# Left tiles of a top-1 expert layer: expert weights split once into 16-bit parts in memory, and left rows grouped by expert over pairs of batches

## The chip, the cores and the metric

The kernel runs on one core of one Trainium2 chip. The metric is the device time of one execution in microseconds (us). The core's engines are called PE (TensorE, matmuls and the weight loads in front of them), ACT (ScalarE), DVE (VectorE), POOL (GpSimd) and SP (which only issues DMAs here). Each engine works through its own instructions in order and waits on semaphores for the others.

## The reference

Agent attention with 49 agents over four batches of 11456 tokens with 128 channels gives one vector per token. A gate picks one of eight experts for each token, and the expert (128 to 1024 to 128, with a relu between) is applied and scaled.

```python
a2k = sm(agents, k)              # softmax of scale * agents @ k^T
agent_v = a2k @ v                # 49 x 128 per batch
q2a = sm(q, agents)
x = (q2a @ agent_v)              # one row of 128 per token, 45824 rows

logits = x @ w_gate
e_idx = np.argmax(logits, axis=1)
gate_w = softmax(logits)[row, e_idx]
eom = 1 / (1 + np.exp(-(x @ w_output_gate)))
for e in range(8):
    mask = e_idx == e
    h = np.maximum(x[mask] @ w1[e], 0)
    out[mask] = gate_w[mask, None] * eom[mask, e, None] * (h @ w2[e])
```

With the reference's inputs nearly all tokens of a batch go to one expert, the batch's dominant one. The others, the left rows, are few: 705 in batch 0 (677 for expert 3, 27 for expert 4, 1 for expert 1), 432 in batch 1 (431 for expert 4, 1 for expert 7), none in batch 2 and 37 in batch 3 (expert 4).

## The kernel before

The **main stream** computes every token with its batch's dominant expert. A batch is 12 units of eight tiles of 128 tokens, the last one short; a unit is two groups of 512 tokens. Per group, `mm1` makes the hidden values in two halves of four PSUM banks (`h`, 512 wide, f16), `relu` writes a 16-bit high part with ACT (`hh`) and a low part with DVE (`hl`), and `mm2` multiplies both with the split second weights (`vv`): a 256-wide product for `hh` and a 128-wide one for `hl` into `y`. `finish` adds the parts with ACT (`ys`) and DVE (`os`), and POOL scales the rows by `smt` ahead of the store. The scores of k and q (`ks`, `qs`), the averages (`av`) and the gate logits (`lg`) are small products that are slipped in between. For q, `q_rest` makes the exponentials `ef`, of which a copy goes to memory (`efd`) together with the token's gate factor in column 49.

The **left rows** are worked out afterwards. `left_table` counts the left rows per group and makes a table of tiles of up to 128 rows of one group; `left_index` finds the tokens of some tiles, and POOL gathers their `ef` rows. `left_load` has SP read the tile's averages (`lav`) and its expert's weights (`lw_ld`, f32, 512 KB each) from memory. `left_front` turns the `ef` rows (`let`, copied by ACT to `let_sb`) and multiplies them with the averages (`lx`, copied to `lxs`). `left_back` makes eight f32 products of 128 columns for the hidden layer (`lh`), relu on ACT, and eight f32 products for the output (`ly`); ACT scales the result, and POOL scatters its rows into `out`. A group is an expert in one batch. `PHASES` fixes the tiles that are laid out in the program: 13 for batches 0 to 2 and one for batch 3; more than these would be worked in a loop at the end.

Nothing of the order is left to the hardware: the builder keeps a clock of its own with a cost for each instruction, and every piece of work is a generator in `streams` with a priority. `tick`, `block` and `idle` let those go on whose operands are ready by that clock, between the instructions of `main_stream`. A changed cost, priority or condition moves instructions on all engines. `left_static` runs two ways of left tiles, `left_scatter` writes their rows, `choose` loads a batch's dominant expert, `kept` writes a batch's averages to memory, and `q_tail` counts.

## Time and profile before

| what | value |
|---|---|
| median of three runs | 976.56 us (976.25 to 977.01) |
| the profiled execution's own time | 976.57 us |
| its span in the trace | 974.8 us |
| mean granted clock of PE | 0.997 |
| first main hidden product (`h`) | 57.3 us |
| first and last left product (`lh`, `ly`) | 779.4 and 965.2 us |
| bytes moved by DMA | 148.63 MB |
| loads of left weights (`lw_ld`) | 28 of 512 KB |

A row of the profile names an engine, an operation, the tiles it writes and reads (out<-in) and its shape as partitions x elements. Since a helper records every operation, all have line 219, and rows are told apart by their tiles. In a row of time the first number is the start in us from the start of the span, the second the time from the first to the last of the xN instructions that it merges, and a bracket names the idle time ahead and what ended it. An f32 product counts as two records. "median" columns of a tile's rows are min/median/max in ns; rows with a bar give busy us in total and mean ns of one, then the idle time before it.

### The profile page before, as it was taken

What the parts mean: (1) busy time and instruction counts of PE and PEld (TensorE: products, weight loads), DVE (VectorE), ACT (ScalarE), POOL (GpSimd) and SP (SyncE); (2) the same over time, 40 slices, a digit from 0 to 9 for tenths busy, and PEclk for the clock granted to TensorE, in tenths of its full rate; (3) what the DMA queues carried; (4) which work ended last, traced back from release to release, by engine and by line L of the source; (5) the groups of instructions that cost most, each with busy time, mean ns of one, the idle gap of its engine ahead of it and who ended that gap; (6) DMA issues with size and microseconds to landing.
All of it is one profiled execution on the core that took longest, in us unless ns stands there. A gap on an engine that the chain in (4) does not pass through costs nothing. (4 is left out here: it accounts for less than half of the span.)

```text
span 974.8 us, 37665 instructions
## 1 busy us (share of the span) xinstructions
PE 953.0 (98%) x15819; PEld 730.4 (75%) x15819; DVE 788.0 (81%) x2119; ACT 590.5 (61%) x1401; POOL 352.5 (36%) x629
## 2 busy tenths in 40 slices
PE   9999999999999999999999999999999999999996
PEld 7867777777777777776777777777777677888885
DVE  2878888989888887889878889889999878678652
ACT  2366666665766666667666666667566566555552
POOL 1013255552232364431323554521234354442221
PEclk9999999999999999999999999999999999999998
DMA  9986655646465655444566545444333453825420
GB/s 332 297 295 162 162 148 156 154 140 172 150 185 155 176 159 137 148 133 146 143 182 172 155 133 161 148 133 135 103 82 83 119 144 96 195 77 163 165 73 29
DMA packets 108899, 148.63 MB, mean 152 GB/s; under 512 B 62595, under 2 KB 71223, under 8 KB 108725
## 3 DMA queue, kind: packets, MB, share of 16 engines
q1 hardware_dynamic: 107380, 144.70, 51.5%
q8 instruction: 125, 2.05, 0.9%
q0 software_dynamic: 1344, 1.49, 0.8%
q14 instruction: 50, 0.40, 0.1%
HBM read 90.88 MB, written 35.17 MB: 129 GB/s over the span
## 5 line engine op out<-in xcount | busy, mean ns | idle before, releaser
L219 PE MATMUL y<-vv,hh 128*128 128x256 f16 (+1 forms) x2880 | 526.6, 273 | 5.2 <-DVE lL L219 2.3
L219 DVE SCALAR_TENSOR_TENSOR hl<-h,hh 128x512 f16<-128x512 f32 (+1 forms) x736 | 448.1, 667 | 93.1 <-ACT hh L219 90.7
L219 PE MATMUL y<-vv,hl 128*128 128x128 f16 (+1 forms) x2880 | 500.0, 219 | 1.5 <-DVE hl L219 0.9
L219 ACT ACTIVATE hh<-h 128x512 f16<-128x512 f32 (+1 forms) x736 | 372.1, 590 | 185.1 <-PE h L219 184.8
L219 PEld LDWEIGHTS <-hh 128*128 128x128 f16 (+1 forms) x2880 | 282.7, 98 | 56.9 <-issue 16.0
L219 PEld LDWEIGHTS <-hl 128*128 128x128 f16 (+1 forms) x2880 | 283.8, 99 | 9.5 <-issue 4.4
L219 PE MATMUL h<-x_ld,w 128*128 128x512 f16 (+1 forms) x1472 | 256.2, 376 | 0.7 <-DVE hl L219 0.4
L219 PEld LDWEIGHTS <-w 128*128 128x128 f16 x1472 | 83.5, 95 | 109.4 <-issue 72.9
L219 POOL TENSOR_TENSOR os<-os,smt 128x512 f32<-128x512 f32 (+1 forms) x91 | 94.9, 1042 | 114.1 <-DVE os L219 65.2
L219 ACT COPY ys<-y 128x256 f32<-128x256 f32 x179 | 67.6, 378 | 103.4 <-PE y L219 101.7
L219 DVE TENSOR_TENSOR os<-y,ys 128x256 f32<-128x256 f32 x179 | 74.2, 414 | 29.2 <-ACT ys L219 25.3
L219 POOL TENSOR_TENSOR e<-ef,e 128x392 f16<-128x392 f32 (+1 forms) x48 | 43.2, 899 | 67.8 <-ACT e L219 67.7
L219 POOL TENSOR_TENSOR ev<-S,km_o 128x400 f32<-128x400 f32 (+1 forms) x36 | 32.8, 914 | 58.2 <-PE av L219 53.9
L219 PEld LDWEIGHTS ks<-at,k_ld 128*32 128x32 f32 (+1 forms) x2316 | 39.9, 116 | 10.3 <-issue 7.8
L219 PE MATMUL ks<-at,k_ld 128*32 128x50 f32 (+1 forms) x2316 | 46.6, 213 | 0.7 <-DMA k_ld<-kT 0.6
L219 PE MATMUL qs<-at,q_ld 128*32 128x50 f32 (+1 forms) x2736 | 43.3, 210 | 0.0
L219 PEld LDWEIGHTS qs<-at,q_ld 128*32 128x32 f32 (+1 forms) x2736 | 36.5, 111 | 9.0 <-issue 8.0
L219 PE MATMUL lh<-lxs,lw_ld 128*128 128x128 f32 x224 | 42.5, 276 | 0.7 <-ACT lh L219 0.6
L219 PE MATMUL ly<-lw_ld,lh 128*128 128x128 f32 x224 | 42.3, 276 | 0.0
L219 POOL TENSOR_SCALAR smt<-lT,i 128x8 f32<-128x8 f32 (+1 forms) x48 | 15.5, 323 | 70.5 <-DVE lT L219 41.6
L219 POOL TENSOR_TENSOR og<-oh,ll 128x64 f32<-128x64 f32 (+1 forms) x48 | 16.3, 340 | 66.7 <-DVE oh L219 47.0
L219 ACT COPY S<-ks 128x400 f32<-128x400 f32 (+1 forms) x48 | 23.5, 490 | 23.2 <-PE ks L219 23.2
(252 smaller groups left out, 1012.8 us busy)
## 6 DMA issues: line engine op xcount, KB each, us to landing
v_ld<-v SPq DMA_DIRECT2D x44, 512.0 KB
q_ld<-qT SPq DMA_DIRECT2D x44, 512.0 KB
out<-os SPq DMA_DIRECT2D x88, 256.0 KB
k_ld<-kT SPq DMA_DIRECT2D x43, 512.0 KB
lw_ld<-w SPq DMA_DIRECT2D x28, 512.0 KB
efd<-ef SPq DMA_DIRECT2D x44, 200.0 KB
x_ld<-x_ld SPq DMA_DIRECT2D x132, 64.0 KB
w1t<-w SPq DMA_DIRECT2D x4, 512.0 KB
```

The lines of the kernel that those rows point to most:

```text
L219: return getattr(self.eng, op)(*a, **k)
```

## The change

1. `PHASES` pairs the batches: phase 0 is batches 0 and 1 with 12 tiles, phase 1 batches 2 and 3 with one. A group is now an expert over both batches of a pair, with the count of the first batch (`cnt0`) kept in the table, so that a row's batch follows from its place (`two`, a 0/1 column per batch). The averages of both batches are one tile of 98 rows, loaded once per phase, and the `ef` row stands in the half of its batch (`xt`, DVE).
2. `halves` reads each expert's two weight matrices once, scales them by a power of two from the sum of squares, splits them into 16-bit high and low parts, and writes them to memory (`w1p`, `w2p`). Three experts are split in each of the batches 0 and 1 and two in batch 2, at priority 3.
3. The left tiles load these parts (the bytes are the same) and use three f16 products instead of one f32 product for the hidden layer, and a 256-wide and a 128-wide one for the output. The values between are split too (`lxs`, `lh`: high part on ACT, low part on DVE), the result is put together by ACT and DVE, and the powers of two are undone in the row factor (`lg`, and `sxi` in `ef`).
4. Priorities: the last q units of batch 3 and the preparing of phase 1 go to 0.

```diff
-PHASES = [(0, 3, 13, 384), (3, 1, 1, 128)]
+PHASES = [(0, 2, 12, 256), (2, 2, 1, 256)]
...
-        yield from ACT.q.copy(avn[0:A], t[0:A, 0:P])
+        sx, state[b]["sxi"] = yield from scale(state[b]["an"], f"sx{b}", 4)
+        yield from ACT.q.activation(avn[0:A], t[0:A, 0:P], AF.Copy, scale=sx[0:A])
...
+    def halves():
+        for e in range(E):
+            while not (clk.started and len(state) > e // 3 and "i12" in state[len(state) - 1]
+                       and (len(state) < B and K.get(len(state), {"v": 0})["v"] < 8) and not urgent[0]):
+                yield None
+            halving[0] = True
+            src, dst = [], []
+            for x in (w1, w2):
+                s = wk.tile([P, F], F32, name=f"hw{len(src)}_{e}", tag="w1t", bufs=2)
+                yield from SY.q.dma_start(s, x[e])
+                src.append(s)
...
+                yield from ACT.q.activation(d[:, 0:F], src[k], AF.Square, accum_out=sq[:, k:k + 1])
...
+            yield from PE.q.matmul(r[:, 0:2], ones, sq, start=True, stop=True)
...
+                yield from ACT.q.activation(full, full, AF.Copy, scale=s[:, k:k + 1])
+                yield from ACT.q.copy(hi, full)
+                yield from POOL.q.tensor_tensor(lo, full, hi, op=ALU.subtract)
+                yield from SY.q.dma_start(x[e], dst[k])
+            halved[0] = e + 1
+            halving[0] = False
...
-        spawn(q_rest(b, u, s, mark))
+        spawn(q_rest(b, u, s, mark), LASTQ if b == B - 1 and u >= 10 else 2)
...
-        yield from POOL.q.tensor_copy(ef[0:pp, 0:nt, A], T)
+        yield from POOL.q.tensor_scalar(ef[0:pp, 0:nt, A], T, state[b]["sxi"][0:pp], None, op0=ALU.mult)
...
-            yield from PE.q.matmul(t[:, 0:n * P], ones[0:ng, :], c[0:ng].rearrange("p n k -> p (n k)"), start=True,
-                                   stop=True)
+            for k in range(n):
+                yield from PE.q.matmul(t[:, k * P:(k + 1) * P], c[0:ng, k, :], ppt[0:ng], start=True, stop=True)
...
-        yield from SY.q.dma_start(w1t, w1[bass.ds(er, 1)].rearrange("a p f -> p (a f)"))
+        yield from SY.q.dma_start(w1t, w1p[bass.ds(er, 1)].rearrange("a p f -> p (a f)"))
...
+        yield from DVE.q.tensor_tensor(xt, ef[:, 0:A].unsqueeze(1).broadcast_to([P, 2, A]),
+                                       two.unsqueeze(2).broadcast_to([P, 2, A]), op=ALU.mult)
...
-        yield from PE.q.transpose(t[0:A, 0:P], ef[:, 0:A], idf)
+        yield from PE.q.transpose(t[0:2 * A, 0:P], xt.rearrange("p b k -> p (b k)"), idf)
...
-        yield from ACT.q.copy(xs, x[:, 0:P])
+        yield from ACT.q.copy(xs[:, 0, :], x[:, 0:P])
+        yield from DVE.q.scalar_tensor_tensor(xs[:, 1, :], x[:, 0:P], 1.0, xs[:, 0, :], op0=ALU.mult, op1=ALU.subtract)
...
-                yield from PE.q.matmul(h[:, j * P:(j + 1) * P], w1t[:, fs], xs, start=True, stop=True)
+                yield from PE.q.matmul(d, w1t[:, f0:f0 + P], xs[:, 0, :], start=True, stop=False)
+                yield from PE.q.matmul(d, w1t[:, f0:f0 + P], xs[:, 1, :], start=False, stop=False)
+                yield from PE.q.matmul(d, w1t[:, F + f0:F + f0 + P], xs[:, 0, :], start=False, stop=True)
...
-            yield from ACT.q.activation(hs, h, AF.Relu)
+            yield from ACT.q.activation(hs[:, 0, :], h, AF.Relu)
+            yield from DVE.q.scalar_tensor_tensor(hs[:, 1, :], h, 0.0, hs[:, 0, :], op0=ALU.max, op1=ALU.subtract)
...
+            yield from PE.q.matmul(y[:, 0:2 * C], hs[:, 0, fs], w2v[:, f, :], start=(f == 0), stop=False)
+            yield from PE.q.matmul(y[:, 0:C], hs[:, 1, fs], w2v[:, f, 0:C], start=False, stop=(f == NB - 1))
-        yield from ACT.q.activation(o, y[:, 0:C], AF.Copy, scale=ef[:, A:A + 1])
+        yield from ACT.q.activation(o, y[:, C:2 * C], AF.Copy, scale=g)
+        yield from DVE.q.scalar_tensor_tensor(o, y[:, 0:C], g, o, op0=ALU.mult, op1=ALU.add)
...
-        while counted[0] < b0 + nb:
+        while counted[0] < (3 if ph == 0 else B) or ph and not prepared[0]:
...
-        for j, n in enumerate((3, 4, 4, 2) if nst > 2 else (nst,)):
+        for j, n in enumerate((4, 4, 4) if nst > 2 else (nst,)):
...
-                while (ph, k) not in ready or i > finished[0]:
+                while (ph, k) not in ready or i > finished[0] or halved[0] < E:
...
-        spawn(left_prepare(ph), 1)
+        spawn(left_prepare(ph), 1 - ph)
...
+    spawn(halves(), 3)
```

Where the instructions stand now. First ACT in batch 1, at the second half of a main group: `hh` are the relus of the main stream, `S` and `ys` copies of scores and outputs, `e` the 16-bit exponentials. Before:

```order
L219 ACTIVATE hh_0_6423<-h_0_0_6400 128x512
L219 ACTIVATE hh_1_6426<-h_0_1_6410 128x512
L219 ACTIVATE hh_2_6429<-h_0_2_6412 128x512
L219 ACTIVATE hh_3_6431<-h_0_3_6417 128x512
L219 CAST e_3_90<-ef_3_6394 128x8x49
L219 COPY S_3_6477<-ks_3_6337 128x400
L219 ACTIVATE hh_4_6538<-h_1_0_6521 128x512
```

And in the changed program, where `hw` is an expert's matrix and `hd` its parts:

```order
L219 ACTIVATE hh_0_6516<-h_0_0_6494 128x512
L219 ACTIVATE hh_1_6519<-h_0_1_6500 128x512
L219 ACTIVATE hh_2_6522<-h_0_2_6502 128x512
L219 ACTIVATE hh_3_6524<-h_0_3_6510 128x512
L219 COPY S_3_6568<-ks_3_6409 128x400
L219 ACTIVATE hw_3_6121<-hw_3_6121,hs_6414 128x1024
L219 CAST hd_3_6126<-hw_3_6121 128x1024
L219 ACTIVATE hh_4_6624<-h_1_0_6608 128x512
```

Two instructions of 1024 columns stand between the two groups of four relus, and the cast of `e` has moved away.

Next PE at the end of the program, from the last products of the main stream on. Before, the second half of one left tile follows (tile 0 of the last phase, whose `let` and `lx` stand earlier), and then the branches of the loop at the end:

```order
L219 MATMUL y_0_21469<-vv_1_15806,hh_7_21427 96x256
L219 LDWEIGHTS hl_7_21428
L219 MATMUL y_0_21469<-vv_1_15806,hl_7_21428 96x128
L219 MATMUL lh_0_0_21508<-lxs_0_21396,lw_00_0_ld 128x128 x4
L219 MATMUL lh_0_1_21519<-lxs_0_21396,lw_00_0_ld 128x128 x4
L219 MATMUL ly_0_21528<-lw_00_0_ld,lh_0_0_21516 128x128 x4
L219 MATMUL ly_0_21528<-lw_00_0_ld,lh_0_1_21525 128x128 x4
```

In the changed program tile 10 of the first phase only starts there with its `lx`:

```order
L219 MATMUL y_0_21790<-vv_1_15990,hh_7_21702 96x256
L219 LDWEIGHTS hl_7_21703
L219 MATMUL y_0_21790<-vv_1_15990,hl_7_21703 96x128
L219 MATMUL lx_10_21818<-let_sb_10_21814,lav_16750 128x128
L219 LDWEIGHTS lw_100_0_ld
L219 MATMUL lh_10_0_21843<-lxs_10_21834,lw_100_0_ld 128x128
```

Behind it come the rest of tile 10, all of tile 11 and all of the last phase's tile; ten left tiles stand ahead of the last main product, where it was 13 before.

Last DVE at the same place in the changed program (there were no left rows on DVE behind the main stream before): the low parts of `lh`, the `xt` products (in `big`, 98 columns) and the outputs (in `big`, from `ly`):

```order
L219 SCALAR_TENSOR_TENSOR lh_10_0_21860<-lh_10_0_21843,lh_10_0_21860 128x512
L219 TENSOR_TENSOR big_8_19745<-big_8_19745,ltwo_8s_8_19908 128x98
L219 SCALAR_TENSOR_TENSOR lh_10_1_21876<-lh_10_1_21863,lh_10_1_21876 128x512
L219 SCALAR_TENSOR_TENSOR lxs_11_21895<-lx_11_21883,lxs_11_21895 128x128
L219 TENSOR_TENSOR lg_11_21902<-big_8_19745,lie_8s_8_20155 128x1
L219 SCALAR_TENSOR_TENSOR big_8_19745<-ly_10_21885,lg_10_21841,big_8_19745 128x128
L219 SCALAR_TENSOR_TENSOR lh_11_0_21933<-lh_11_0_21906,lh_11_0_21933 128x512
L219 SCALAR_TENSOR_TENSOR lh_11_1_21949<-lh_11_1_21936,lh_11_1_21949 128x512
L219 SCALAR_TENSOR_TENSOR big_8_19745<-ly_11_21952,lg_11_21902,big_8_19745 128x128
L219 TENSOR_TENSOR bigs_0_21243<-bigs_0_21243,ltwo_0s_0_21385 128x98
```

The `xt` of the last tile (the last row) stands behind the output of tile 11.

More of the change, by code (lines that the diff above doesn't have):

```diff
@@ L390, in agent_attention_top1_moe @@
         gss.append(t)
+    ls = cp.tile([2 * E, P + 2], F32, name="ls")
+    side, expert, sign = ls[:, 0:P], ls[:, P:P + 1], ls[:, P + 1:P + 2]
     oht = []
@@ L1401, in left_table @@
         yield from PE.q.matmul(cn_[:, 0:ng], ones, tt_, start=True, stop=True)
-        cnt = row("cntsb")
-        yield from DVE.q.tensor_copy(cnt, cn_[:, 0:ng])
+        cnt, cnt0 = row("cntsb"), row("cnt0")
+        yield from DVE.q.tensor_copy(cnt0, cn_[:, 0:E])
+        yield from DVE.q.tensor_tensor(cnt, cn_[:, E:2 * E], cnt0, op=ALU.add)
         release(mark)
@@ L1504, in left_index @@
         yield from DVE.q.tensor_tensor(inv, r, tb[:, :, 2], op=ALU.is_ge)
+        two = lt("ltwo" + own, [rows_, 2], nm, [n, 2])
+        bt = two[:, :, 1]
+        yield from DVE.q.tensor_tensor(bt, r, tb[:, :, 4], op=ALU.is_ge)
+        yield from DVE.q.tensor_scalar(two[:, :, 0], bt, -1.0, 1.0, op0=ALU.mult, op1=ALU.add)
+        ppx = col("ppx")
+        yield from DVE.q.tensor_tensor(ppx, bt, tb[:, :, 4], op=ALU.mult)
+        yield from DVE.q.tensor_tensor(r, r, ppx, op=ALU.subtract)
+        if not own:
+            yield from DVE.q.tensor_tensor(pb1, pb1, pb[:, 0, :], op=ALU.subtract)
+            yield from DVE.q.scalar_tensor_tensor(pb[:, 0, :], pb1, bt, pb[:, 0, :], op0=ALU.mult, op1=ALU.add)
         rb = r.unsqueeze(2).broadcast_to([P, n, P])
@@ L1600, in left_front, with left_back @@
         mark = hold()
-        yield from PE.q.matmul(x[:, 0:P], av[0:A], et[0:A], start=True, stop=True)
-        xs = wk.tile([P, P], F32, name=f"lxs{nm}", tag="l_xs")
-        yield from ACT.q.copy(xs, x[:, 0:P])
+        yield from PE.q.matmul(x[:, 0:P], av[0:2 * A], et[0:2 * A], start=True, stop=True)
+        xs = wk.tile([P, 2, P], F16, name=f"lxs{nm}", tag="l_xs")
+        yield from ACT.q.copy(xs[:, 0, :], x[:, 0:P])
+        yield from DVE.q.scalar_tensor_tensor(xs[:, 1, :], x[:, 0:P], 1.0, xs[:, 0, :], op0=ALU.mult, op1=ALU.subtract)
         release(mark)
-        return xs
-    def left_back(nm, xs, w1t, w2t, o, ef, tag="lh"):
+        g = wk.tile([P, 1], F32, name=f"lg_{nm}", tag="l_g", bufs=3)
+        yield from DVE.q.tensor_tensor(g, ef[:, A:A + 1], ie, op=ALU.mult)
+        return xs, g
+    def left_back(nm, xg, w1t, w2t, o, tag="lh"):
+        xs, g = xg
+        w2v = w2t.rearrange("p (f k) -> p f k", k=2 * C)
         hidden = []
```

186 lines of the change are left out of this document (118 added, 68 removed).

## The prediction

> **What bounds the kernel now.** I read the page first (busy shares, slices), then what TensorE waited for, then the windows of the last third, then single rows of time.
>
> ```profile
> span 974.8 us, 37665 instructions
> PE 953.0 (98%) x15819; PEld 730.4 (75%) x15819; DVE 788.0 (81%) x2119; ACT 590.5 (61%) x1401; POOL 352.5 (36%) x629
> PE y L219 <- DVE lL L219: 2.3, 4, 0.7
> 660.00:757.00 97.00, 95.55 (x1322) 69.64 (x1319) 91.11 (x264) 61.83 (x150) 31.76 (x60) 1.00 0.37 99
> 757.00:961.50 204.50, 202.00 (x2149) 161.71 (x2146) 145.54 (x425) 115.22 (x276) 78.00 (x118) 1.00 0.42 124
> 961.50:974.80 13.30, 4.01 (x35) 3.69 (x32) 0.76 (x3) 2.18 (x5) 1.01 (x1) 0.75 0.10 32
> ```
>
> PE is busy 98% of the span. A busy PE may still have gaps, since the ends of matmuls are modelled, but its longest total wait for any one thing is 2.3 us (the third row). So PE's instructions, one behind the other, set the time until 961.5, and what is taken from PE shortens the kernel as long as its suppliers keep up. The window rows give for each stretch the busy time of PE, weight loads, DVE, ACT and POOL. The left tiles fall into the stretch from 757 on. There DVE is busy 145.5 of 204.5 us; just before, it was 91.1 of 97 (94%) and PE still 95.6, so a DVE at 94% does not by itself hold PE up. Behind 961.5 lies a tail of 13.3 us with 4 us of PE in it.
>
> **The change, part by part.** The price of one product is read from how far apart the starts stand.
>
> ```profile
> 924.92 0.27 PE L219 MATMUL y<-vv,hh 128*128 128x256 f16 x1
> 925.03 0.27 PE L219 MATMUL let<-kc,big 128*49 128x128 f32 x1
> 925.14 0.22 PE L219 MATMUL y<-vv,hl 128*128 128x128 f16 x1
> 925.19 0.27 PE L219 MATMUL y<-vv,hh 128*128 128x256 f16 x1
> 925.30 0.39 PE L219 MATMUL ly<-lw_ld,lh 128*128 128x128 f32 x2
> 925.52 0.22 PE L219 MATMUL y<-vv,hl 128*128 128x128 f16 x1
> 925.58 0.27 PE L219 MATMUL y<-vv,hh 128*128 128x256 f16 x1
> ...
> 926.36 0.27 PE L219 MATMUL y<-vv,hh 128*128 128x256 f16 x1
> 926.56 0.49 PE L219 MATMUL lx<-let_sb,lav 49*128 49x128 f32 x2
> 926.98 0.23 PE L219 MATMUL y<-vv,hl 128*128 128x128 f16 x1
> 927.04 0.27 PE L219 MATMUL y<-vv,hh 128*128 128x256 f16 x1
> ```
>
> A 256-wide f16 product holds PE 0.11 us (925.19 to 925.30), a 128-wide one 0.056 (925.14 to 925.19, 926.98 to 927.04). An f32 `ly` product between them adds 0.22, `let` 0.11; `lx` adds 0.62 - 0.11 = 0.51.
>
> *Removed from PE* ahead of the last main product: 13 left tiles of 16 f32 products, 13 x 16 x 0.22 = 45.8 us (46.2 unrounded at 0.222), and 14 times `let` and `lx`, 14 x 0.62 = 8.7. Together **54.9 us**.
>
> *Added there.* A tile now takes 8 times three 128-wide f16 products (8 x 0.168) and 8 pairs of 256 and 128 (8 x 0.165): 2.66 us where it took 3.55. By the order of the changed program (shown above) only **ten** of the 13 tiles stand ahead of the last main product: 26.6 us. No row shows three 128-wide products with new weights in a line; the ends are 0.056 and 0.11 (half of the f32 pair), and I take 0.056, since an `hl` row has the same shape and new weights. `let` with 98 columns lies between 0.11 and 0.22, `lx` with 98 rows between 0.22 (a full f32 product) and 0.51; I take 0.22 twice: 4.6 us for 11 and 10 of them. Eight `hr` sums at 0.22 are 1.8. The 13 products of `pb` have the columns of the four they replace. Net: 54.9 - 26.6 - 4.6 - 1.8 = **-21.9 us**, so the last main product, at 961.5 now, would start at 939.6.
>
> The Trainium skill's page "TensorE: Matmul & The Clock Gate", section "Back-to-back issue gap", speaks against this term: a sustained stream of weight load and product pairs takes about 81 ns each at 128 columns, so three would cost 243 ns, more than the f32 product's 222. The rows above, with new weights at each product, show 56 ns; by the page's figure the ten tiles would take 34.6 us and the sum would be 8 us worse.
>
> *The splitting of the weights* puts ACT, POOL and SP work beside the first half of the main stream.
>
> ```profile
> L219 ACT ACTIVATE vv<-w2t x8: 612/638/650, 53.7 to 669.7; 128x512 f16<-128x512 f32 x8
> L219 ACT ACTIVATION_READ_ACCUMULATOR vv<-w2t x8: 185/208/221, 54.2 to 670.3; 128x1 f32 x8
> L219 ACT ACTIVATE vv<-w2t,s_s x8: 707/726/766, 57.1 to 677.8; 128x512 f16<-128x512 f32 x8
> L219 ACT COPY S<-ks 128x400 f32<-128x400 f32 x44 | 22.5, 512 | 23.2 <-PE ks L219 23.2
> L219 ACT COPY lL<-lg 128x128 f32<-128x128 f32 x44 | 12.2, 277 | 4.6 <-PE lg L219 4.4
> L219 POOL TENSOR_TENSOR ev<-S,km_o 128x400 f32<-128x400 f32 x33 | 31.7, 963 | 54.7 <-PE av L219 50.5 <-DVE a L219 3.7 <-DVE km_o L219 0.6
> L219 POOL TENSOR_TENSOR ll<-lL,rr 128x128 f32<-128x128 f32 x44 | 17.8, 404 | 34.1 <-DVE rr L219 33.7 <-DVE lT L219 0.3
> ...
> 445.61 2.07 ACT L219 ACTIVATE hh<-h 128x512 f16<-128x512 f32 x4 [2.23 <-PE h L219]
> 447.54 0.65 ACT L219 ACTIVATE wsq<-w1t 128x512 f16<-128x512 f32 x1
> 448.77 0.39 ACT L219 COPY ys<-y 128x256 f32<-128x256 f32 x1
> 450.65 0.60 ACT L219 ACTIVATE hh<-h 128x512 f16<-128x512 f32 x1 [1.49 <-PE h L219]
> ```
>
> ACT copies cost (512 - 277) / 272 = 0.86 ns a column, so 1024 columns are 0.44 us dearer than 512: a square 1.08 + 0.21 for its sum, a scaling 1.17, a cast about 1.1. An expert is 7.1 us of ACT, eight are 57; ACT would rise from 590 to about 650 busy us, far from full. POOL costs (963 - 404) / 272 = 2.05 ns a column, a subtraction 2.2 us, sixteen 36; POOL is at 36%. The 16 MB that SP moves more lie beside DMA rows at about half load, and the 44 `ef` products on POOL that replace copies cost 0.13 us each beside the same cover. What matters is ACT's order. The work mostly stands in **blocks** of two (two squares 2.6 us, scaling and cast 2.3), three per expert, 24 in all, between two groups of four relus, and behind a block queue `ys`, `hh`, and then DVE's `hl`, which frees PE's banks. The rows from 445 on show such a place: relus end at 447.7, the next group starts at 450.65, ACT had waited 1.49 us for PE again after 1.4 us of squares and a `ys`. The room is thus 2.9 us less 0.4: a block fits. Where `S` (0.51) or an `e` (0.55) shares the place it is 0.5 to 1 us late. From nothing to 24 x 1.0 = 24 us; I take 0.12 a block, **+3 us**, because most places have that room. Below nothing it cannot go, since PE loses no work by it.
>
> *DVE in the left part* gets two `lh` low parts (0.68 each), one of `lxs` and one of the output (0.35 each) and a product for `xt` (0.25): 2.3 us a tile, 23 us for ten. 145.5 + 23 over 204.5 - 21.9 is 92%, under the 94% that PE bore before. 0 to 5 us; I take **+1**.
>
> *The tail.* The order rows show what stands behind the last main product: now the second part of one tile whose front is done, then three whole tiles one behind the other.
>
> ```profile
> L219 DVE SCALAR_TENSOR_TENSOR hl<-h,hh 128x512 f16<-128x512 f32 x704 | 438.9, 682 | 92.2 <-ACT hh L219 89.8 <-issue 0.2
> L219 ACT ACTIVATE hh<-h 128x512 f16<-128x512 f32 x704 | 364.2, 602 | 181.6 <-PE h L219 181.6
> L219 ACT COPY lxs<-lx 128x128 f32<-128x128 f32 x14 | 3.8, 274 | 6.9 <-PE lx L219 6.9
> L219 ACT COPY let_sb<-let 49x128 f32<-49x128 f32 x14 | 3.7, 261 | 1.6 <-PE let L219 1.4
> L219 DVE TENSOR_TENSOR bigs<-bigs,lrs x1: 293/293/293, 921.2 to 921.2; 128x128 f32<-128x128 f32 x1
> ...
> 961.46 0.22 PE L219 MATMUL y<-vv,hl 128*96 128x128 f16 x1
> 961.72 0.36 ACT L219 ACTIVATE ys<-y,smt 96x128 f32<-96x128 f32 x1 [2.27 <-PE y L219]
> 962.18 0.35 DVE L219 SCALAR_TENSOR_TENSOR os<-y,smt,ys 96x128 f32<-96x128 f32 x1 [2.27 <-ACT ys L219]
> 965.60 0.37 ACT L219 ACTIVATE bigs<-ly,bigs 128x128 f32<-128x128 f32 x1 [1.45 <-PEq L1745]
> 966.78 1.01 POOL L219 DMA_INDIRECT out<-bigs,ltg_0s  x1 [5.75 <-SPq L1745]
> ```
>
> Now 5.3 us pass from the last main product (961.46) to the last scatter (966.78). In the change I count from that product. From PE to ACT takes 0.04 (961.68 to 961.72), from ACT to DVE 0.10. First tile: `lx` 0.45, behind the two engines' work for the last `y` the cast and the low part, so `lh` runs from 1.5. One tile from there: first half 12 x 0.056 and drain 0.22, relu at 0.9 for 0.6, low part 1.6 to 2.3; second half's low part to 3.0, since DVE does them in a row; then the second half of `ly`, 0.66 and drain: 3.8 us. The first tile's DVE also does the next tile's `xt` in between: `ly` ends at 5.9. The second tile follows at 6.05 and ends at 9.85; its output needs ACT 0.37 and DVE 0.35 (to 10.7). Only then DVE does `xt` of the last tile: 0.25, `let` 0.38, copy 0.26, `lx` 0.37, cast 0.27, low part 0.35 and handovers 0.4 bring `lh` to 12.95, `ly` to 16.75, the output to 17.6, the scatter to 17.7. That is 17.7 - 5.3 = **+12.4 us**, between 9 (no handovers, `xt` in time) and 16 (other waits in the same queues). The last tile's weights are issued by SP behind the store of the last `os` (done at 1.9), some 10 us before they are used. From the scatter to the end nothing changes.
>
> The clock in the last window is 0.75 of full. The same page, section "The HAM clock gate", says that the clock halves after an idle window of about 3.4 us; the longest stretch here with only `let` and `lx` in it is 3.1 us, so I leave the clock full; halved for the last tile it would cost some 2 us, inside the upper bound.
>
> *Sum*: -21.9 + 3 + 1 + 12.4 = **-5.5 us**, a span of 969.3. The profiled execution took 976.57 us, 1.8 around its span, and the median of the runs is 976.56; so the forecast is **971.1 us**.
>
> **The rivals.**
>
> *ACT's blocks hold PE up* (slower). Place: the 24 places between relu groups. From 0.12 + 5.5 / 24 = 0.35 us a block the gain is gone. For it: behind a late relu stands DVE's `hl`, behind that the banks of the next `h`. Against it: the room of the wsq place. At 0.5 a block it adds 9 us: **980**.
>
> *The tail hides and nothing stalls* (faster). Tail at 9, no other loss: 976.6 - 21.9 + 9 = **964**. For it: PE's tiny waits now. Against: the order of DVE's rows.
>
> *16-bit products are no cheaper*. At 0.11 for each 128-wide one a tile takes 8 x (0.33 + 0.22) = 4.4 us, 17 more for ten: **988**. The `hl` rows speak against it; this is the page's rule above, which with 81 ns would give 979.
>
> *The regrouping does not fit*: from the reference's inputs, 12 tiles for the first pair and 1 for the second just fill the fixed ones. A tile too many would run in the loop behind the end, at over 17 us for a chain like the tail's: over 988.
>
> **How the numbers follow.** Forecast 0.52 (967 to 975.5 by its own bounds), ACT's blocks 0.22, hidden tail 0.18, dear products 0.05, overflow 0.03. A measurement here can tell 0.2% (2 us) from no change. Faster: 0.18 and 0.43 of the forecast, 0.61. Same: 0.07 of the forecast and 0.08 of the first rival with small prices, 0.15. Slower: the rest, 0.24. The range from 963.5 to 981.5 takes in the hidden tail and most of the first rival.
>
> **What would show it.** 128-wide f16 `lh` starts 0.056 us apart (0.11: the third rival). The last main product near 943.6: later means stalls, and the gaps in PE should then stand behind relus that follow `hd` and `hw` on ACT. The last scatter 17.7 us after that product: much less is the second rival. Left tiles after the fixed ones would show the fourth. The forecast is wrong most easily in the size of the tail and of the blocks, each some 4 us.

## The result, and the profile after

The changed kernel takes **990.6 us** (median of four runs, 988.96 to 992.81); the kernel before, run beside it, 976.4 (976.1 to 977.01). The ratio is 1.0148, with a 95% interval of 1.0136 to 1.0160: slower, where 971.1 was forecast. The profiled execution of the change took 992.81 us, 1.8 of it around the span.

The page's first rows:

```profile
span 991.0 us, 37853 instructions
PE 949.1 (96%) x15819; PEld 716.8 (72%) x15819; DVE 828.3 (84%) x2245; ACT 632.2 (64%) x1459; POOL 394.9 (40%) x661
```

And the windows that match those of before (the stretch ahead of the left part, the left part, the tail), with the same columns:

```profile
684.00:775.90 91.90, 90.23 (x1174) 65.37 (x1174) 83.89 (x247) 56.93 (x138) 32.82 (x60) 0.98 0.32 85
775.90:961.80 185.90, 177.15 (x2090) 133.85 (x2089) 161.83 (x487) 105.82 (x256) 69.64 (x105) 1.00 0.42 122
961.80:991.00 29.20, 14.97 (x157) 12.11 (x155) 7.79 (x23) 6.97 (x18) 5.03 (x5) 0.81 0.16 55
```

DVE rose by 40 us, ACT and POOL by 42 each, and none of the three is full. Yet in the left part PE has 8.8 us in which it is not busy (185.90 - 177.15), where it had 2.5 of 204.5 before, and the tail is 29.2 us instead of 13.3. The left part does get shorter, but it starts late, and it ends late.

Busy shares hide where the lost time lies, because the ends of matmuls are modelled. So I compared the *starts* of PE's products in both traces: for each pair of neighbouring shapes the usual distance counts as work, and what lies beyond it as idle time (products that run slower at half clock count as idle time too). At four points, after against before:

| point | start before | start after | shift | of it work | of it idle |
|---|---|---|---|---|---|
| 1025th main hidden product (late in batch 2) | 660.9 | 675.0 | +14.1 | +0.2 | +13.9 |
| last main hidden product | 956.0 | 956.3 | +0.3 | -23.0 | +23.2 |
| last main product | 961.46 | 963.94 | +2.5 | | |
| last scatter | 966.78 | 981.79 | +15.0 | | |

The 1025th product lies behind all splitting, of which the last instruction ends at 545 us; the first of batch 3 is the 1105th. The work did go: 23 us. But 13.9 us of idle time come in batches 0 to 2, where the weights are split (4.7 in batch 0, 5.4 in batch 1, some 4 in batch 2, and none in stretches without splitting), 9.3 more between the 1025th and the last hidden product, and the tail is 17.85 us long (963.94 to 981.79) instead of 5.32. From the last scatter to the end of the span it is 9.25 us instead of 8.02. So +2.5 + 12.5 + 1.2 = +16.2, which is 992.81 - 976.57.

The waits of PE over the whole kernel (total us, times, longest):

```profile
PE y L219 <- DVE lL L219: 3.9, 5, 1.0
PE y L219 <- ACT S L219: 3.6, 3, 1.3
PE h L219 <- DVE hl L219: 2.7, 11, 0.4
...
PE qs L219 <- issue: 2.0, 1, 2.0
```

There is no one large wait: many of about a microsecond, for several producers. And not all of the lost time is a wait (columns of the windows as above, the row of time between them):

```profile
725.00:730.00 5.00, 5.00 (x40) 3.18 (x38) 4.96 (x10) 2.93 (x7) 2.06 (x3) 1.00 0.60 165
...
729.90 0.48 PE L219 MATMUL pbs<-pptsb,big 16*128 16x128 f32 x2
...
730.00:735.00 5.00, 5.00 (x32) 3.13 (x33) 2.93 (x10) 1.55 (x3) 2.10 (x4) 0.66 0.23 59
```

PE is busy throughout, but from 730.7 on the clock is half for 3.4 us, which costs 1.7. No wait over 0.25 us stands in the 9 us ahead of it. What does stand there is the last of four `pbs` products of the left index, the `pb` products of the prediction. In seven other runs with the regrouping a stretch at half clock begins within 1.1 us of the fourth product of such a group (the eighth in e8_tail), with no wait over 0.5 us ahead; it never does in the two kernels with the old, wider products (before and e16_split_alone). Not each group of four is followed by one, and why it comes stays open.

Rows of time from the tail:

```profile
965.30 1.44 PE L219 MATMUL lh<-lxs,lw_ld 128*128 128x128 f16 x23 [0.28 <-DVE lxs L219]
...
975.83 2.69 PE L219 MATMUL lh<-lxs,lw_ld 128*128 128x128 f16 x24 [0.35 <-ACT lxs L219]
978.31 2.41 PE L219 MATMUL ly<-lw_ld,lh 128*128 128x256 f16 x16
...
981.79 0.98 POOL L219 DMA_INDIRECT out<-bigs,ltg_0s  x1 [6.51 <-DVE more L219]
```

Here 23 `lh` products take 1.44 us, their starts 0.056 apart; most of the last tile's start 0.107 apart, at half the clock.

### The profile page after: what moved, and what is told of

Its sections match the earlier page's. It is cut to its first block, busy times and chain, and to the rows that moved or that the text cites. A ratio compares the mean times of both kernels' runs of the same rounds, so it can differ in the third digit from the quotient of the medians.

```text
span 991.0 us, 37853 instructions
## 1 busy us (share of the span) xinstructions
PE 949.1 (96%) x15819; PEld 716.8 (72%) x15819; DVE 828.3 (84%) x2245; ACT 632.2 (64%) x1459; POOL 394.9 (40%) x661
## 3 DMA queue, kind: packets, MB, share of 16 engines
q0 software_dynamic: 1248, 1.44, 0.8%
## 4 chain that ended last, share of the span: by engine, by line
PE 70%; DVE 18%; ACT 7%; DMA 2%; issue 2%; POOL 0%; POOLq 0%; SPq 0%; ACTq 0%; DVEq 0%
PE y L219 36%; PE h L219 17%; DVE hl L219 10%; ACT hh L219 4%; PE ks L219 3%; PE qs L219 3%; PE av L219 2%; PE warm L219 2%; PE ly L219 1%; DVE os L219 1%; ACT hd L219 1%; PE avT L219 1%; PE lh L219 1%; DVE a L219 1%; PE lg L219 1%
## 5 line engine op out<-in xcount | busy, mean ns | idle before, releaser
L219 POOL TENSOR_TENSOR hd<-hw,hd 128x1024 f16<-128x1024 f32 x16 | 34.2, 2137 | 14.0 <-ACT hd L219 14.0
L219 POOL TENSOR_TENSOR sm<-sm,ev 128x400 f32<-128x400 f32 (+1 forms) x33 | 32.2, 977 | 11.2 <-ACT ev L219 11.2
L219 PE MATMUL lh<-lxs,lw_ld 128*128 128x128 f16 x312 | 33.7, 225 | 1.8 <-ACT lxs L219 0.7
```

Of the source, the lines that this page charges most:

```text
L219: return getattr(self.eng, op)(*a, **k)
```

## The experiments

All times are medians beside the kernel before, which stood at 975.9 to 976.7 throughout (the ratio is to that of the same chip). "Shift" is that of the 1025th main hidden product (660.9 before), "tail" the time from the last main product to the last scatter (5.32 before); these three are read from the one profiled execution of each run.

| run | us | ratio (95%) | shift | last main product | tail |
|---|---|---|---|---|---|
| the change | 990.61 | 1.0148 (1.0136 to 1.0160) | +14.1 | 963.94 | 17.85 |
| e1_no_split | 978.75 | 1.0024 (1.0014 to 1.0033) | +2.9 | 952.32 | 16.93 |
| e2_moves | 979.04 | 1.0035 (1.0022 to 1.0047) | +2.1 | 950.04 | 17.93 |
| e3_pieces | 990.24 | 1.0138 (1.0121 to 1.0155) | +14.7 | 964.51 | 17.93 |
| e4_pool | 995.82 | 1.0199 (1.0182 to 1.0216) | +21.6 | 972.12 | 17.98 |
| e5_dve_low | 989.02 | 1.0137 (1.0120 to 1.0154) | +9.2 | 957.89 | 17.85 |
| e6_pool_alone | 980.68 | 1.0059 (1.0040 to 1.0078) | +4.8 | 952.79 | 16.93 |
| e7_act_alone | 984.75 | 1.0098 (1.0073 to 1.0123) | +6.7 | 955.87 | 17.93 |
| e8_tail | 989.20 | 1.0144 (1.0127 to 1.0161) | +13.0 | 972.30 | 5.24 |
| e9_late | 996.39 | 1.0195 (1.0177 to 1.0213) | +15.3 | 969.64 | 17.82 |
| e10_late_dve | 995.72 | 1.0193 (1.0176 to 1.0210) | +12.0 | 965.94 | 17.86 |
| e11_late_front | 990.82 | 1.0140 (1.0123 to 1.0157) | +12.8 | 974.23 | 7.06 |
| e12_group32 | 987.96 | 1.0115 (1.0100 to 1.0131) | +1.9 | 972.78 | 5.29 |
| e13_group32_gap | 986.16 | 1.0097 (1.0083 to 1.0111) | +1.9 | 971.32 | 5.30 |
| e14_no_low | 986.76 | 1.0101 (1.0086 to 1.0117) | +2.3 | 958.46 | 18.98 |
| e16_split_alone | 986.68 | 1.0103 (1.0087 to 1.0118) | +10.0 | 972.10 | 5.42 |
| e17_prios | 998.04 | 1.0217 (1.0204 to 1.0231) | +13.9 | 970.56 | 17.29 |
| e18_group32_lastq | 981.59 | 1.0050 (1.0036 to 1.0063) | +1.4 | 966.37 | 5.33 |
| e19_group32_prios | 991.83 | 1.0161 (1.0142 to 1.0180) | +1.6 | 964.89 | 16.86 |

### Which part of the splitting costs the time

First the change without any splitting, then with its transfers alone (the edit of the first, cut; the second keeps the loop over all experts and loads and stores their weights in it):

```diff
-        for e in range(E):
+        for e in range(1):
...
+                yield from POOL.q.memset(d, 0.001)
+                for x in (w1p, w2p):
+                    yield from SY.q.dma_start(x[0], d)
```

> The splitting of the weights is left out: one constant tile is written to memory once and every left tile loads that in place of its expert's parts, so the left rows' values are not the reference's; all else as changed. Theory A (the long ACT instructions of the splitting hold relus up): the 1025th of the 1472 main hidden products, 660.9 us before and 675.0 in the changed kernel, is back within 1 us of 660.9, and the whole takes 990.6 - 14 = 975 to 978 us. Theory B (the 16 MB of moves and SP's queue hold the main stream's loads up): the same. Theory C (the stalls come from the new order of q_rest, sxi and the priorities, not from the splitting): 990 us, product at 674 to 676. The tail stays 17.5 to 18 us from the last main product to the last scatter.

> As the run without splitting, but all 16 weight matrices are loaded and stored again at the places of the splitting, with nothing computed on them. Theory A: the 1025th main hidden product within 1.5 us of 660.9, the whole 975 to 979 us. Theory B: product at 674 to 676, the whole 988 to 992 us. A share of both: between.

Without splitting the shift falls from 14.1 to 2.9 us, with the 16 MB of transfers alone it is 2.1. So the transfers alone add nothing to the shift, and some 12 of the 14 us come with the work on engines; the other 2 to 3 are there without any splitting. It also shows that even a splitting for nothing would not have made the change faster: 23 us less work on PE, and still 1.0024.

Then ACT's instructions in four pieces, the scaling and the cast moved to POOL, and POOL's part moved to DVE (which also takes one of ACT's two instructions away, since DVE then reads the unscaled weights):

```diff
+                for j in range(4):
+                    c = slice(256 * j, 256 * (j + 1))
+                    yield from ACT.q.activation(d[:, c], src[k][:, c], AF.Square, accum_out=sq4[:, k, j:j + 1])
...
+                    yield from POOL.q.tensor_scalar(full[c], full[c], s[:, k:k + 1], None, op0=ALU.mult)
+                    yield from POOL.q.tensor_copy(hi[c], full[c])
...
-                yield from ACT.q.copy(hi, full)
-                yield from POOL.q.tensor_tensor(lo, full, hi, op=ALU.subtract)
+                yield from ACT.q.activation(hi, full, AF.Copy, scale=s[:, k:k + 1])
+                    yield from DVE.q.scalar_tensor_tensor(lo[c], full[c], s[:, k:k + 1], hi[c], op0=ALU.mult,
+                                                          op1=ALU.subtract)
```

> The changed kernel with each of the six ACT instructions of 1024 columns per expert cut into four of 256 (about 0.3 us each, 0.5 with the sum's read); the results are the same. Theory A: a relu waits at most 0.5 us instead of 1.3, so of the 14 us some 3 to 6 stay: the product at 664 to 667, the whole 980 to 984 us. Theory B or C: 674 to 677 and 989 to 993 us (the pieces add some 0.2 us of ACT each, 96 more pieces in all, beside PE).

> Scaling and cast of the weights on POOL in pieces of 512 columns, only the squares on ACT in pieces of 256. Theory A: little is left on ACT, the product at 662 to 666, the whole 977 to 982 us, unless POOL's own work (some 50 us more) holds the outputs' scaling and the exponentials up. Theory B or C: 674 to 677 and 989 to 993 us.

> The changed kernel with the low parts of the weights on DVE in pieces of 512 columns, straight from the weights and the scale, so that ACT loses its separate scaling and POOL has no subtraction; the results are the same. Theory D: no 2-us POOL instruction is left, DVE has some 18 us more of its own work; the product at 664 to 669, the whole 979 to 984 us. Theory A: ACT has 19 us less of long instructions, which would give some 5 us: 669 to 671, the whole 984 to 987 us.

That ACT's *long instructions* stand in the way of its short ones was my first theory, and e3_pieces refutes it: in pieces a quarter as long, the splitting costs the same. A place in that kernel shows why. PE's waits between 481 and 490 us:

```profile
PE y L219 <- ACT S L219: 1.9, 1, 1.9
```

And ACT's rows of time there:

```profile
480.86 0.44 ACT L219 ACTIVATE hd<-hw 128x256 f16<-128x256 f32 x1
...
482.43 2.06 ACT L219 ACTIVATE hh<-h 128x512 f16<-128x512 f32 x4 [1.04 <-PE h L219]
484.35 0.30 ACT L219 COPY lL<-lg 128x128 f32<-128x128 f32 x1
484.50 0.57 ACT L219 ACTIVATE ef<-qz 128x392 f32<-128x392 f32 x1
...
485.18 0.58 ACT L219 CAST e<-ef 128x392 f16<-128x392 f32 x1
485.60 0.54 ACT L219 COPY S<-ks 128x400 f32<-128x400 f32 x1
```

The last piece is done at 481.4, and ACT even waits 1.04 us for PE then. But in the order that the builder makes around the pieces, `lL`, `ef`, `ys` (left out here) and `e` stand in one row behind the next four relus, and `S`, for which PE waits, is the last of them. At this place what counts is into which gap the added work pushes the rest, not the length of one instruction.

e4_pool took work from ACT and gave it to POOL, and became 5 us *slower*. At one place its shift grows from 2.2 to 10.2 us. DVE's rows there:

```profile
202.36 0.16 DVE L219 SCALAR_TENSOR_TENSOR a<-se,d 128x8 f32<-128x8 f32 x1
202.62 6.14 DVE L219 SCALAR_TENSOR_TENSOR a<-eo,a 128x8 f32<-128x8 f32 x1
208.68 1.87 DVE L219 SCALAR_TENSOR_TENSOR hl<-h,hh 128x512 f16<-128x512 f32 x3
```

POOL's first and last row of the eight that stand there without a gap, and what became of PE:

```profile
201.33 1.56 POOL L219 TENSOR_SCALAR hw<-hw,hs 128x512 f32<-128x512 f32 x1
...
207.59 1.14 POOL L219 TENSOR_TENSOR hd<-hw,hd 128x512 f16<-128x512 f32 x1
...
209.41 0.38 PE L219 MATMUL h<-x_ld,w 128*128 128x512 f16 x1 [3.05 <-DVE hl L219]
```

The windows there (columns as above):

```profile
205.00:210.00 5.00, 1.74 (x18) 1.26 (x16) 5.00 (x4) 0.91 (x2) 3.73 (x5) 0.97 0.37 142
210.00:215.00 5.00, 4.96 (x24) 2.51 (x24) 4.21 (x12) 2.20 (x5) 3.49 (x7) 0.50 0.10 28
```

A DVE instruction on 8 columns takes 6.14 us; the median of its kind is 0.17, and the longest of before's 48 took 1.04. It ends when POOL's eight end (207.59 + 1.14 = 208.73). Behind it wait `hl` and, for 3.05 us, PE, and behind that wait the granted clock is half for a stretch (0.50 in the second window). The Trainium skill's page "SBUF — State Buffer", section "Who interferes with whom", has a rule that fits: a DVE instruction with two SBUF inputs contends with a GpSimd instruction that reads SBUF, and the lock on what they share is exclusive. The rows agree, and show more: DVE stayed out until eight POOL instructions in a row were done, three of them the splitting's. In the change itself the same thing happens on a smaller scale:

```profile
492.49 2.13 POOL L219 TENSOR_TENSOR hd<-hw,hd 128x1024 f16<-128x1024 f32 x1
492.62 2.01 DVE L219 SCALAR_TENSOR_TENSOR a<-eo,a 128x8 f32<-128x8 f32 x1
494.88 2.48 DVE L219 SCALAR_TENSOR_TENSOR hl<-h,hh 128x512 f16<-128x512 f32 x4
...
496.81 0.24 PE L219 MATMUL h<-x_ld,w 128*128 128x192 f16 x1 [0.36 <-DVE hl L219]
497.40 0.44 PE L219 MATMUL h<-x_ld,w 128*128 128x192 f16 x5 [0.35 <-DVE hl L219]
```

The POOL subtraction of the splitting, an eight-column instruction of DVE that ends when it ends (494.63), a late `hl`, a late `h`. With POOL's part on DVE (e5_dve_low) the shift in the profiled execution falls from 14.1 to 9.2. That execution was the fastest of its runs, 985.9 us; their median, 989.0, is within the interval of the change. And ACT has less to do there too, so the 4.9 us can't be put down to POOL alone.

Last, ACT's and POOL's parts each alone, on unsplit data and beside the transfers:

> As the run with moves alone (no splitting on ACT, left tiles load a constant), plus the 16 subtractions of 1024 columns on POOL at the places of the splitting, their result unused. Theory D (a POOL instruction holds up DVE instructions with two operands in SBUF until it ends, so a subtraction of 2.14 us stops DVE, behind which the low parts `hl` queue): the 1025th main hidden product, 663.0 us with moves alone and 675.0 in the changed kernel, comes at 667 to 673, with DVE instructions of 128x8 or 128x64 of up to 2.1 us beside the subtractions; the whole 983 to 989 us. Theory A (ACT): 662 to 665 and 978 to 981 us.

> As the run with moves alone, plus the six ACT instructions of 1024 columns per expert, their results unused and nothing of the splitting on POOL, DVE or PE. Theory D: the product at 662 to 666, the whole 978 to 982 us. Theory A: 669 to 675 and 985 to 991 us. If both POOL alone and ACT alone give about half of the 12 us, both count.

Against e2_moves POOL's part alone costs 1.6 us of total time and 2.7 of shift, ACT's 5.7 and 4.6. Together they cost 12 of shift. That is more than the sum of 7.3, by 4.7 us. Up to the 641st product (experts 0 to 5) the sum is nearly right, 10.9 against 3.7 and 6.1; the rest comes with the last two experts. PE's eight `hr` sums, about 1 us, are in neither run. What is also new when both run is a chain: POOL's subtraction waits in order for ACT's cast, and POOL's own work behind it waits too. The rows of this tile in the change, the second of them from the list of who waited for it:

```profile
L219 POOL TENSOR_TENSOR hd<-hw,hd x16: 2126/2134/2167, 89.7 to 542.4; 128x1024 f16<-128x1024 f32 x16
...
  POOL hd L219: 14.0, 6
```

The second row says that POOL sat idle 14.0 us in six waits for the cast; three of them, 6.2 us, stand at the last two experts. That these waits are the missing 4.7 us was not tried by itself.

### Splitting at another time

> The changed kernel with one condition more: the splitting of an expert begins only once the next batch's k scores are all copied, which moves it from the first to the later part of each batch. Theory E (the splitting costs where ACT and DVE also carry the copies and maxima of the k scores: in the changed kernel experts 4 and 5, split at 303 to 376 us behind those scores, added nothing to the main stream, experts 3, 6 and 7 some 3 to 5 us): the 1025th main hidden product at 663 to 668 instead of 675, the whole 980 to 985 us. Theory F (an expert costs 1.5 us wherever it is put): 673 to 677 and 989 to 992 us.

> The same place, and the low parts of the weights on DVE instead of POOL. If POOL's subtractions still hold DVE up there (POOL is busier in that part of a batch, 10 of 20 us against 5 to 7), it gains 1 to 4 us on the run with only the new place: product at 662 to 666. If DVE's own 18 us weigh more: product later by 1 to 5 us than in that run.

> The run with the new place, plus the left part: the front of a way's next tile may begin before its tile is done, the last phase's index no longer waits for the first phase's, and PE gets a left row's transposition 0.8 us after DVE's product for it. By the order of the program two tiles' last products then stand behind the last main product, no front. Expected: the last scatter 6 to 8 us behind the last main product instead of 17.9, the last main product 5 to 8 us later than in the run with only the new place, the whole 3 to 7 us less than that run's. If the tail's gain is given back in PE's waits for left tiles as in the run with the tail alone (989.2 against 990.6): within 2 us of it.

```diff
-                       and (len(state) < B and K.get(len(state), {"v": 0})["v"] < 8) and not urgent[0]):
+                       and (len(state) < B and K.get(len(state), {"k": 0})["k"] >= NU and K[len(state)]["v"] < 12) and not urgent[0]):
```

Splitting only when the scores of k are done leaves the shift at 15.3, and the total gets worse, so it is not these scores alone that the splitting collides with. With POOL's part on DVE (e10_late_dve, the same edit as in e5_dve_low) the total is no better. e11_late_front adds an earlier front of the left tiles, so that its tail is 7 us; the left part pays for it (974.23 for the last main product).

### Each half of the change alone

e16_split_alone adds the splitting to the kernel before, and nothing reads its parts. e12_group32 has the regrouping without the splitting, with f32 products on the unsplit weights:

> The splitting alone: the kernel before with all experts' weights split at the places of the change, and the parts never read. If the splitting costs 11.6 us by itself (990.6 against 979.0 us with moves alone): 986 to 989 us, the 1025th main hidden product at 671 to 676. If its cost comes from meeting the other new work: under 983 us.

> The regrouping alone: 12 tiles and one over pairs of batches, as in the change, but the left products stay f32 on the unsplit weights, so there is no splitting and no low part on DVE in the left tiles; the results are the same. One tile less is 3.55 + 0.62 = 4.2 us of PE; `let` with 98 columns and its wait for DVE's product may take 0 to 3 us back. By the order of the program only the last phase's tile stands behind the last main product, as before. Theory G (the regrouping pays, the 16-bit form doesn't): 972 to 976 us, the last scatter 5 to 6 us behind the last main product. Theory H (the losses of the left part come with the regrouping): 977 to 981 us.

**Splitting alone costs 10 us** of total time (1.0103), all of it ahead of the 1025th product, and behind that nothing is regained. **Regrouping alone costs 11** (1.0115), though it *removes* 4.3 us of PE's work: between the 1025th and the last main hidden product, 13.2 us of idle time appear. So idle time in the left part needs neither 16-bit products nor splitting. In e12_group32 some of it has an address. DVE's rows around 895 and the `pexc` row of PE:

```profile
895.36 3.47 DVE L219 TENSOR_TENSOR_SCAN cum<-ones,oht 128x90 f32<-128x90 f32 x8 [0.83 <-POOL oht L219]
898.75 0.66 DVE L219 SCALAR_TENSOR_TENSOR hl<-h,hh 128x512 f16<-128x512 f32 x1
899.33 0.16 DVE L219 COPY tot<-cum 128x8 f32<-128x8 f32 x1
...
899.63 0.37 PE L219 MATMUL pexc<-tot,kc 128*128 128x16 f32 x2 [2.40 <-DVE tot L219]
```

And two windows:

```profile
895.00:900.00 5.00, 2.60 (x31) 2.27 (x30) 4.64 (x11) 2.33 (x5) 2.54 (x5) 1.00 0.63 216
900.00:905.00 5.00, 5.00 (x37) 2.84 (x35) 3.15 (x14) 1.25 (x4) 0.00 (x0) 0.66 1.05 233
```

The eight scans of batch 3's left table stand ahead of `hl`, PE has already been given the product `pexc` that needs their result, and everything behind it on PE waits 2.4 us. The clock then drops to 0.66 of full in the next window, which costs 1.7 us more (0.34 of 5). The scans come that early because of the change's fourth part, priority 0 for the last units of q, as the next runs show. A second address is a wait of 1.9 us of `tbs` for `big` at 774, again with half a clock behind it (774.5 to 777.9); it is there in the three runs that follow from this one too, but not in the change.

Three runs start from this one. e13_group32_gap puts 0.8 us between the product `xt` on DVE and the `let` that waits for it. e18_group32_lastq also undoes `LASTQ`, e19_group32_prios the other new priority as well. e17_prios undoes both in the whole change:

```diff
+        yield from pause(800.0)
...
-    LASTQ = 0
+    LASTQ = 2
...
-        spawn(left_prepare(ph), 1 - ph)
+        spawn(left_prepare(ph), 1)
```

> The same with PE given a left row's transposition 0.8 us after DVE's product for it. If the new wait of `let` for DVE costs what it shows in the run with the tail alone (6.3 us of late `let` for 13 tiles), this gains 1 to 4 us on the regrouping alone; if other work moves into the wait's place, within 1 us of it.

> The regrouping alone, in 32-bit products and with the gap ahead of let (986.2 us, ratio 1.0097), with the first of the two priorities undone: the second halves of batch 3's last score tiles at priority 2 again. Nothing is left out. Theory K: the 2.6-us wait of pexc for tot behind the eight scans goes, with it the stretch at half clock behind it, about 4 us together, so 982 us, ratio 1.005 to 1.007. Theory L: the wait only moves, 1.008 to 1.011.

> As the kernel before it (regrouping alone, 32-bit, gap), with both priorities undone: the preparation of the second group at 1 too. Nothing is left out. Its order leaves a whole left tile (let, lx, lh, ly) behind the last main product, where the one before it leaves lh and ly, so the end is about 2 us later by that. Theory K: as the kernel before it or up to 2 us more, 1.005 to 1.009. Theory L: 1.010 to 1.013. If it is below the one before it in spite of the end, the second priority costs idle time too.

> The changed kernel with its two new priorities undone: the second halves of batch 3's last score tiles run at priority 2 again (not 0), and the preparation of the second group of left tiles at 1 (not 0). Nothing is left out. Theory K (the priorities of part 4, which the prediction did not price, push the scans and the index arithmetic of the left rows ahead of h's operands on VectorE and cause the 9 us of TensorE idle time that come after the first product of batch 3): the idle time between that product and the last main product falls from 9 to 5 us or less, and the ratio from 1.015 to 1.010 or less. Theory L (the left tiles' chains of small operations cost it at any priority): idle time and ratio stay as they are, 1.013 to 1.016.

The gap gives 1.8 us, though the intervals of the two ratios overlap. Undoing `LASTQ` gives **4.6** (986.16 to 981.59), as theory K said. With the gap the scans come at 904 and PE's wait for `tot` is still there, at 907.5; with `LASTQ` undone they come at 914.9 and `pexc` at 922.5, without a wait. First e13_group32_gap, then the windows of e18_group32_lastq around `pexc`:

```profile
PE pexc L219 <- DVE tot L219: 2.6, 1, 2.6
905.00:910.00 5.00, 2.27 (x15) 1.71 (x16) 4.90 (x19) 0.52 (x2) 0.00 (x0) 0.84 0.50 118
910.00:915.00 5.00, 4.86 (x37) 3.33 (x36) 2.94 (x12) 2.93 (x7) 0.00 (x0) 0.82 0.06 9
...
915.00:920.00 5.00, 4.97 (x52) 3.96 (x49) 5.00 (x12) 2.59 (x7) 2.21 (x3) 1.00 0.74 258
920.00:925.00 5.00, 4.66 (x49) 3.72 (x50) 3.48 (x13) 2.93 (x8) 0.00 (x0) 1.00 0.34 90
```

The other priority, though, is needed, against both theories. e19_group32_prios has its last main product earlier by 1.5 us, and then this (the last tile's weights in SP's queue, the gather of its rows on POOL, and two rows of PE):

```profile
968.40 0.94 SPq L219 DMA_DIRECT2D lw_ld<-w  x2
968.41 1.06 POOL L219 DMA_INDIRECT bigs<-efd,ltu_0s  x1 [3.81 <-issue]
...
973.77 0.42 PE L219 MATMUL let<-kc,bigs 128*98 128x128 f32 x1 [8.66 <-issue]
975.70 3.52 PE L219 MATMUL lh<-lxs,lw_ld 128*128 128x128 f32 x16 [0.36 <-ACT lxs L219]
```

The second group's index is worked out so late that its rows are gathered from 968.41 on, behind the main stream. DVE's `xt` waits for them until 973.41, and PE with it, 8.7 us in the tail. In the whole change undoing both costs 7.4 us, where theory K had expected 5 us of gain. The changed kernel shows no `pexc` wait to begin with, and the new order makes others (1.7 us of `tbs` waiting for `big`, with the clock at 0.86 and 0.80 behind it, and 1.8 of `y` waiting for `os`). So theory K holds for the regrouping alone, and there for one of the two priorities. In the whole change undoing both doesn't remove the 9 us, and `LASTQ` was not undone there by itself.

### DVE's low parts, and the tail

> The run without splitting, with DVE's low parts of the left tiles left out and their high parts used in their place, so that PE has the same products and DVE some 2 us less per tile (the left rows are not the reference's). Theory I (DVE's low parts hold the main stream up in the left part): PE's idle time between the 1217th and the last main hidden product, 7.5 us over that of before without splitting, falls to 4 or less, the whole to 973 to 977 us. Theory J (it is the waits of the left tiles for one another and the order): idle 6 to 8 us over, 977 to 980 us.

> The changed kernel with the splitting as it is, but the three groups of left tiles found beside one another, and each way allowed to begin the front of its next tile before the tile before it is done. By the order of the program only the products of the last phase's tile then stand behind the last main product. If the tail is a serial chain of waits: two tiles' products (2 x 2.7 us) and three fronts move ahead of the last main product, which comes at about 971 instead of 963.9, and the last scatter 5 to 6 us behind it instead of 17.9; the whole 984 to 987 us. If the left tiles were late for another reason (DVE full), the last main product comes later by as much as the tail gains: 989 to 992 us.

e14_no_low takes the three low-part instructions of each left tile from DVE (from e1_no_split). If DVE's added load caused the idle time of the left part, it should fall. It rose, from 8.3 us to 15, and the time by 8 us. What did that is open: the builder made another order from the changed instructions, and less work became a slower kernel.

e8_tail brings the three tiles forward, by working out three index groups in parallel and starting a front one tile ahead. The tail is 5.24 us, as short as before. The kernel is hardly faster (the interval of its ratio contains that of the change), because the last main product is 8.4 us later. From the 1025th product to there it takes 9.5 us longer than the change. Some 6 of these are the products of the moved tiles, PE work wherever they stand. The rest is the size of 3.4 us lost to the clock: behind its first `pbs` products it is half from 731.4 to 741.7, three times as long as in the change. And `let` waits for DVE in the stream (PE's waits from 700 to 970 us):

```profile
PE let L219 <- DVE big L219: 2.2, 4, 1.1
...
PE let L219 <- ACT lh L219: 1.1, 2, 0.6
PE let L219 <- issue: 1.0, 2, 0.6
```

No version came below the kernel before. The fastest that computes everything is e18_group32_lastq at 981.6 us, 0.5% slower.

## Why the prediction was wrong

The forecast was 971.1; replaced term by term, it becomes the measured 992.8 of the profiled execution: 971.1 + 1.1 + 10.9 + 8.3 + 0.1 + 1.2 = 992.7.

- **Removed from PE: right.** -21.9 was forecast up to the last main product. Measured are -23.0 up to the last main *hidden* product and 2.2 us of left products between that and the last main one, so -20.8 (+1.1). Three 128-wide f16 products with new weights do start 0.056 us apart; the third rival is refuted here. The 81 ns that the Trainium skill's page "TensorE: Matmul & The Clock Gate", section "Back-to-back issue gap", gives for this were not seen. The `pb` products, put at nothing because their columns are the same, are not quite that: they hold PE 5.4 us where the old ones took 4.0, besides the half clock behind the first four. The left rows fitted the fixed tiles, so the fourth rival didn't occur.
- **The splitting: the right place, the wrong size.** "I take 0.12 a block, +3 us, because most places have that room" is the step that failed most: 13.9 us of idle time come in its place. Some 2 of them are there without splitting (a shift of 2.1 in e2_moves), so the splitting's own part is about 12, 0.5 a block; added to the kernel before it is 10.0. The first rival, at 0.5 a block, had this term, though not the time, 980. Two things were wrong behind the number. The room was read from one place, where ACT had a square, a `ys` and nothing else to do between relus. Where `S`, `lL`, `ef` and `e` share the place, the backlog comes out one relu group later (e3_pieces). And I counted POOL at "36%", as if a POOL instruction had no effect on another engine. It holds up DVE's short instructions with two SBUF inputs (2.0 us at 492.62), and `hl` stands behind them; POOL's part alone costs 2.7 us of shift.
- **DVE in the left part: wrong.** "92%, under the 94% that PE bore before" gave +1; 9.3 us appeared, with DVE at 87% (161.83 of 185.90). A busy share says whether an engine has room, not whether the one result that PE waits for next stands in front of or behind the others. And the step counted the wrong items: without DVE's low parts the idle time is not smaller (e14_no_low), and without any 16-bit part it is 13.2 us (e12_group32). It comes with the regrouping, and where that stands alone, a part of it depends on what stands ahead of what on DVE: I had listed the priorities as part 4 of the change and never priced them. There one of them is worth 4.6 us, and the other 10 the other way. In the whole change 1.7 of the 9.3 is the half clock behind `pbs`; for most of the rest the cause stays open.
- **The tail: right in size, in part by luck**, +12.4 forecast and +12.5 measured (17.85 us against 17.7). It includes the halved clock of the last tile, behind no wait longer than 1.1 us, that I had left out at "some 2 us"; the rest was thus 2 us shorter than counted. What I did not see is that this term was mostly not loose time to be won: in e8_tail the tail's products cost some 6 us inside the stream, and idle time there takes 3 more.
- **"From the scatter to the end nothing changes": off by 1.2 us.** Over all runs this stretch has two lengths, 7.7 to 8.5 us and 9.3 to 9.6; e7_act_alone, e8_tail, e10_late_dve, e11_late_front and e17_prios have the long one too. Its cause is open.

The size of the error is that of two added works costed from the free space that an average or one good place shows. Both costs, 10.9 and 8.3 us over, look alike where a place could be read: small pieces in front of an operand of PE.

## What to carry to other kernels

Where one engine is 98% busy behind four others, price added work on the others per place, with what else queues there, and not by their busy shares: here ACT at 61% and POOL at 36% did not take some 40 us more each without 10 to 14 us of stalls on PE. Price priorities like instructions: one line of them moved the regrouping alone by 4.6 and one by 10 us. And before bringing a tail forward, split it into waiting and work; only the waiting can be won.

## What the hardware showed unexpectedly

- POOL instructions without a gap kept a DVE instruction of 128x8 with two SBUF inputs from finishing for 6.14 us (e4_pool; 0.17 is its median), over several of them.
- A wait of PE of 2 to 3 us can bring a stretch at half clock behind it. The changed kernel has one at 277, its longest, whose releaser the profile does not show; the windows around it:

```profile
275.00:280.00 5.00, 3.02 (x91) 2.49 (x90) 2.80 (x15) 2.83 (x11) 1.54 (x6) 1.00 0.77 168
280.00:285.00 5.00, 5.00 (x42) 3.72 (x40) 1.71 (x12) 0.64 (x2) 1.41 (x6) 0.66 0.73 199
```

PE's 2.0 us of busy time missing in the first row are followed by a clock of 0.66 in the second, some 1.7 us: this stall costs nearly twice its length. The stretches at half clock last 3.4 us, or two or three times that (6.8 behind e4_pool's wait, 10.2 in e8_tail). In the stream they came behind waits of 1.4 (e9_late at 558) to 3.05 us (e4_pool), but three waits of 2.1 us were followed by none (e8_tail at 278, e9_late at 246, e14_no_low at 774), and eight runs have one behind `pbs` products without a wait. So a wait of 2 us is a risk of 1.7 more, not a sure price.

The Trainium skill's page "TensorE: Matmul & The Clock Gate", section "The HAM clock gate", puts the drop behind an idle window of about 3.4 us. No run here has a wait that long ahead of a drop in the stream, so for a guess at a stall's price the Trainium skill's figure is too kind.

- Such waits of 1 to 2 us among the score products (`qs`, `ks`), for which no releaser is shown, appear in the change and in e8_tail, e17_prios, e2_moves and e16_split_alone, shorter ones in e5_dve_low and e4_pool. All of these are among the thirteen runs that load the weights beside the main stream; in the seven that don't there is none. Whether the transfers bring them was not tried, and they stay open.
